# A feed-forward kernel's opening loads: the first transposed tile alone, and part of the first weights on another queue

## The chip, the cores and the metric

The kernel runs on 1 core of one Trainium2 chip. The metric is the device time of one execution in microseconds (us); the median of several runs is compared. Engines are named as in the profile: PE is TensorE's matmul, PEld its weight load, ACT ScalarE, DVE VectorE, POOL GpSimd, SP SyncE. SPq and ACTq are the DMA issues on SyncE's and ScalarE's queues.

## What is computed

```python
# x: 1 x 2048 x 640, w1: 640 x 1728, w2: 1728 x 640, all bf16
h = jnp.einsum("bsd,df->bsf", x, w1)
h = silu(h)
out = jnp.einsum("bsf,fd->bsd", h, w2)
```

## The kernel before, in words

**Tiling.** The 2048 tokens are cut into four chunks of 512. The inner size 640 is five k-tiles of 128 (`DT`). The hidden size 1728 is thirteen f-tiles of 128 (`FT`) and a rest of 64. x arrives transposed: `xT[:, k, c0:c1]` holds k-tile k of a chunk, 128 partitions by 512 tokens, and is filled by DMA transposes straight from DRAM. "Tile k" in this text is that k-tile for the first chunk. w1 lies in `w1s[:, k, f]`; "slab k" is its k-th tile, of which the first eight f-tiles (1024 columns, 256 KB) are loaded first.

**The first product.** One block is one f-tile with one k-tile: two matmuls of 64 columns of w1 each (`step`, lines 183 to 187), which run side by side into the two halves of a PSUM bank. The first chunk is special. `opening` (197 to 205) goes through the k-tiles in the outer loop and through eight f-tiles in the inner one, each f-tile in its own bank, so that work can begin when only tile 0 and part of slab 0 have landed. It waits for tile 0 and the first part of slab 0, then for the rest of slab 0 ahead of f-tile `NA`, then in `sweep` for slab and tile k. The fifth k-tile follows at 208 to 211, where each f-tile ends in a SiLU on ACT. After that come f-tiles 8 to 12 of the first chunk, and the three other chunks with the f-tile in the outer loop.

**The second product.** It reads the activated `hT` and w2 and runs on PE to the end; ACT and DVE copy the banks out, SP stores them. The change does not touch it.

**What stands before the first block.** DVE clears a small tile `z` (line 125), and PE multiplies it with itself: 13 dummies of 128 columns and 256 moving columns, and one more as two halves of 64 (`first_dummies`, 135 to 138). Their result is never used. ACT meanwhile loads its table and runs one small SiLU (`warm_up`).

**The order of the loads.** `early` moves an instruction ahead of its engine's part in the barrier at the program's start, so these loads are issued at once. SP's queue takes, in the order of lines 123 to 157: tiles 0 and 1 in one transpose; f-tiles 5 to 7 of slab 0 (`ld_w1b`); slab 1; slab 2; tile 2; slab 3; tiles 3 and 4 in one transpose; slab 4; f-tiles 8 and 9 of all slabs (`ld_rest`); the remaining columns (`ld_rest2`). ACT's queue takes f-tiles 0 to 4 of slab 0. After the barrier SP issues 15 transposes for the other chunks (163) and the loads of w2. A queue issues in its own order, and each DMA has its semaphore, for which `wait` makes an engine stand. The semaphore `s_pe` counts the work that PE announces with `tick`; before the change the dummies announce none.

Of the kernel before, what the change touches and what calls it, by code (L numbers as in the profile page):

```python
# [9 lines left out]
def bass_standalone__dense_activation_silu__prompt_kernel(  # L10
# [13 lines left out]
    P = 128  # L24
    NB = 8
    BANK = 512
    DT = D // P
    FT = F // P
    FL = F - FT * P
    SCH = 512  # L30
    HB = 256
# [7 lines left out]
    pe, act, dve, pool, sp = nc.tensor, nc.scalar, nc.vector, nc.gpsimd, nc.sync  # L39

    with ExitStack() as es:
        def sb(name, shape, dtype):
            return es.enter_context(nc.sbuf_tensor(name, shape, dtype))
# [10 lines left out]
        z = sb("z", [P, HB], bf16)  # L54
        ps = es.enter_context(nc.psum_tensor("ps", [P, NB, BANK], fp32))
# [4 lines left out]
        def sem(name):  # L60
            s = es.enter_context(nc.semaphore(name))
            count[s.name if hasattr(s, "name") else name] = 0
            return [s, 0]

        def tick(ins, s, n=1):
            ins.then_inc(s[0], n)
            s[1] += n
            return (s, s[1])

        def wait(eng, *points):  # L70
            for pt in points:
                if pt is None:
                    continue
                s, v = pt
                key = (id(eng), id(s))
                if seen.get(key, 0) < v:
                    eng.wait_ge(s[0], v)
                    seen[key] = v

        s_pe, s_act, s_dve = sem("s_pe"), sem("s_act"), sem("s_dve")  # L80
# [4 lines left out]
        def load(eng, out_ap, in_ap):  # L85
            s = sem(f"s_ld{n_dma[0]}")
            n_dma[0] += 1
            return tick(eng.dma_start(out=out_ap, in_=in_ap), s, 16)

        def turned(c0, c1, k0, k1):  # L90
            s = sem(f"s_tr{n_dma[0]}")
            n_dma[0] += 1
            return tick(sp.dma_start_transpose(
                out=xT[:, k0:k1, c0:c1], in_=xf[c0:c1, k0 * P:k1 * P]), s, 16)

        ET = mybir.EngineType

        def early(emit, engine, arrived=True):
            n = len(nc.main_func.blocks[0].instructions)
            r = emit()  # L100
            lst = nc.main_func.blocks[0].instructions
            new = lst[n:]
            del lst[n:]
            at = next(
                i for i, ins in enumerate(lst)
                if ins.opcode == ("EventSemaphore" if arrived else "Drain") and ins.engine == engine
            )
            lst[at:at] = new
            return r
# [2 lines left out]
        w2_v = w2[0:F0, :].rearrange("(ft p) d -> p ft d", p=P)  # L112

        NO = NB
        NA = 5
        CO = NO * P

        def slab(eng, k, f0=0, f1=NO):
            return load(eng, w1s[:, k, f0 * P:f1 * P], w1_v[:, k, f0 * P:f1 * P])

        ld_w1 = {}
        ld_t = {}
        ld_t[0] = ld_t[1] = early(lambda: turned(0, SCH, 0, 2), ET.SP, False)
        ld_w1[0] = early(lambda: slab(act, 0, 0, NA), ET.Activation, False)
        p_z = early(lambda: tick(dve.memset(z[:, :], 0.0), s_dve), ET.DVE, False)  # L125

# [2 lines left out]
        def dummies(n, w):  # L129
            for _ in range(n):  # L130
                for c0 in range(0, P, w):
                    pe.matmul(ps[c0:c0 + w, 3, 0:HB], lhsT=z[:, 0:w], rhs=z[:, :],  # L132
                              start=True, stop=True)

        def first_dummies():
            wait(pe, p_z)
            dummies(13, P)
            dummies(1, HC)

        p_warm = early(lambda: tick(pool.memset(warm[:, :], 0.0), s_pool), ET.Pool, False)  # L140
# [4 lines left out]

        early(warm_up, ET.Activation, False)

        ld_w1b = early(lambda: slab(sp, 0, NA, NO), ET.SP, False)
        ld_w1[1] = early(lambda: slab(sp, 1), ET.SP, False)
        ld_w1[2] = early(lambda: slab(sp, 2), ET.SP, False)  # L150
        ld_t[2] = early(lambda: turned(0, SCH, 2, 3), ET.SP, False)
        ld_w1[3] = early(lambda: slab(sp, 3), ET.SP, False)
        ld_t[3] = ld_t[4] = early(lambda: turned(0, SCH, 3, DT), ET.SP, False)
        ld_w1[4] = early(lambda: slab(sp, 4), ET.SP, False)
        CM = CO + 2 * P
        ld_rest = early(lambda: load(sp, w1s[:, :, CO:CM], w1_v[:, :, CO:CM]), ET.SP, False)
# [17 lines left out]
        def mm(o, l, r, start, stop, shared=False):  # L174
            return pe.matmul(o, lhsT=l, rhs=r, start=start, stop=stop, skip_group_check=shared)  # L175
# [7 lines left out]
        def step(b, k, ft, c0, c1, start=False, stop=False):  # L183
            for h0 in (0, HC):
                ins = mm(ps[h0:h0 + HC, b, :], w1s[:, k, ft * P + h0:ft * P + h0 + HC],
                         xT[:, k, c0:c1], start, stop, shared=True)
            return ins
# [9 lines left out]
        def opening():  # L197
            first_dummies()
            wait(pe, ld_t[0], ld_w1[0])
            for ft in range(NO):  # L200
                if ft == NA:
                    wait(pe, ld_w1b)
                part(0, ft, 0, SCH, start=True)
            for k in range(1, DT - 1):
                sweep(k, 0, SCH, ld_w1[k], ld_t[k])
# [16 lines left out]
        for ft in range(NO, FT):  # L222
# [3 lines left out]
            for k in range(DT):  # L226
                ins = step(b, k, ft, 0, SCH, start=(k == 0), stop=(k == DT - 1))
            silu(hT[:, ft, 0:SCH], ps[:, b, :], b, tick(ins, s_pe))
        for c in range(1, NSC):
            wait(pe, ld_xc[c])  # L230
            for ft in range(FT):
                b = bank()
                for k in range(DT):
                    ins = step(b, k, ft, c * SCH, (c + 1) * SCH, start=(k == 0), stop=(k == DT - 1))
                h_last = silu(hT[:, ft, c * SCH:(c + 1) * SCH], ps[:, b, :], b, tick(ins, s_pe))
        h_tail = []
        for q in range(NSC // 2):
            b = bank()
            for k in range(DT):
                for hh in range(2):  # L240
                    c = 2 * q + hh
                    ins = mm(ps[hh * FL:(hh + 1) * FL, b, :], w1s[:, k, F0:F],
                             xT[:, k, c * SCH:(c + 1) * SCH],
                             start=(k == 0), stop=(k == DT - 1), shared=True)
# [130 lines left out]
        for u, eng in ((A, dve), (B, act), (C, act), (E, dve), (G2, act)):  # L375
            for ft in range(FT):
                ins = u.whole(ft, ft == FT - 1)
# [30 lines left out]
```

## Time and profile before

| | us |
|---|---|
| median of 3 runs (lowest, highest) | 124.72 (124.39, 125.12) |
| span of the profiled execution, first to last instruction | 123.8 |
| last semaphore resets in its trace, after the first instruction | 124.7 |
| first dummy on PE | 0.39 |
| first real matmul | 3.82 |
| PE busy in all | 121.3 |

The page gives the profiled execution's span, and no other time of it. The loads that the first sweeps wait for, in that execution (issue is the start of the DMA's issue; landed is when its semaphore was full; wanted is when the first weight load that waits for it started):

| load | queue | issue us | landed us | wanted us |
|---|---|---|---|---|
| tiles 0 and 1 | SP | 0.00 | 3.78 | 3.82 |
| slab 0, f-tiles 0 to 4 (160 KB) | ACT | 0.12 | 2.86 | 3.82 |
| slab 0, f-tiles 5 to 7 (96 KB) | SP | 1.39 | 5.24 | 5.53 |
| slab 1 (256 KB) | SP | 2.00 | 5.88 | 6.52 |
| slab 2 | SP | 2.49 | 6.59 | 8.25 |
| tile 2 | SP | 2.97 | 7.15 | 8.25 |
| slab 3 | SP | 4.17 | 8.23 | 9.97 |
| tiles 3 and 4 | SP | 4.79 | 9.24 | 9.97 |
| slab 4 | SP | 6.07 | 10.55 | 11.70 |
| f-tiles 8 and 9 of all slabs | SP | 6.69 | 12.51 | 13.43 |

How to read the profile: a timeline line has the start, the time, the engine, the line of the kernel, the operation, its tiles and how many were joined; in brackets stands how long the engine was idle before and what ended that. The chain of waits is followed back from the last instruction to what released each step. Matmuls are pipelined, so a matmul's own time is longer than the distance between the starts of two.

### The profile page before, as it was taken

To read this page: it belongs to the slowest core of one execution; us is meant where nothing else is said; L and a number is where in the kernel's file an instruction comes from. 1 tells how busy PE (TensorE), PEld (TensorE's weight loads), DVE (VectorE), ACT (ScalarE), POOL (GpSimd) and SP (SyncE) were. 2 spreads that over 40 slices of the span, in tenths; PEclk is the share of its full clock that TensorE was granted. 3 is DMA by queue.
4 is the path that set the end of the run, shared out by engine and by line. 5 is a ranking of instruction groups with operands and counts; after the bars stand their busy time and mean duration, and the time that the engine had idled before them with its cause. 6 is when DMAs were issued, how large, how long until landed. Compare 5 with 4: busy or idle time off the path is not lost.

```text
span 123.8 us, 2298 instructions
## 1 busy us (share of the span) xinstructions
PE 121.3 (98%) x1056; PEld 58.9 (48%) x1057; DVE 6.9 (6%) x11; ACT 38.8 (31%) x67; POOL 0.3 (0%) x5
## 2 busy tenths in 40 slices
PE   8999999999999999999999999999999999999993
PEld 5345545545545545545544444444444444444452
DVE  0000000000000000000000022002200300222001
ACT  4000985555555555555530011001100200110110
POOL 0000000000000000000000000000000000000000
DMA  6999974554894000000000004302200220023112
GB/s 138 239 246 331 138 86 91 100 77 107 214 394 157 0 0 0 3 5 0 0 0 5 0 0 101 74 0 105 107 0 5 106 106 0 5 106 116 53 66 82
DMA packets 19625, 10.42 MB, mean 84 GB/s; under 512 B 13728, under 2 KB 19104, under 8 KB 19616
## 3 DMA queue, kind: packets, MB, share of 16 engines
q1 hardware_dynamic: 19472, 10.11, 34.1%
q10 hardware_dynamic: 144, 0.16, 0.6%
q8 instruction: 8, 0.13, 0.5%
q14 instruction: 1, 0.01, 0.0%
HBM read 4.51 MB, written 2.62 MB: 58 GB/s over the span
## 4 chain that ended last, share of the span: by engine, by line
PE 95%; DMA 3%; ACT 0%; issue 0%
PE ps L175 95%; DMA xT<-in_x_dram 3%; ACT o_sb L256 0%
## 5 line engine op out<-in xcount | busy, mean ns | idle before, releaser
L175 PE MATMUL ps<-xT,w1s 128*64 128x512 bf16 x540 | 59.6, 384 | 0.1
L175 PE MATMUL ps<-w2s,hT 64*128 64x512 bf16 (+3 forms) x376 | 46.0, 369 | 0.2 <-issue 0.2
L175 PEld LDWEIGHTS ps<-xT,w1s 128*64 128x64 bf16 x540 | 30.0, 111 | 29.6 <-issue 1.2
L179 ACT ACTIVATE hT<-ps 128x512 bf16<-128x512 f32 x52 | 30.0, 607 | 29.9 <-PE ps L175 29.9
L175 PEld LDWEIGHTS ps<-w2s,hT 64*128 64x128 bf16 (+1 forms) x377 | 21.0, 95 | 24.2 <-issue 0.2
L256 ACT CAST o_sb<-ps 128x512 bf16<-128x512 f32 (+1 forms) x9 | 5.0, 551 | 41.5 <-PE ps L175 41.5
L175 PE MATMUL ps<-hT,w2s 64*128 64x512 bf16 x104 | 11.7, 376 | 0.0
L175 PEld LDWEIGHTS ps<-hT,w2s 64*128 64x128 bf16 x104 | 5.0, 94 | 6.3 <-issue 0.4
L254 DVE CAST o_sb<-ps 128x512 bf16<-128x512 f32 (+1 forms) x8 | 5.4, 675 | 40.5 <-PE ps L175 40.5
L254 DVE CAST oT<-ps 128x512 bf16<-128x512 f32 x2 | 1.4, 692 | 74.2 <-PE ps L175 74.2
L256 ACT CAST oT<-ps 128x512 bf16<-128x512 f32 x2 | 1.2, 586 | 10.6 <-PE ps L175 10.6
L132 PE MATMUL ps<-z 128*128 128x256 bf16 (+1 forms) x15 | 3.3, 419 | 0.4 <-DVE z L125 0.4
L175 PE MATMUL ps<-w2t,hTt 64*128 64x512 bf16 (+2 forms) x17 | 2.9, 363 | 0.0
L132 PEld LDWEIGHTS ps<-z 128*128 128x128 bf16 (+1 forms) x15 | 1.9, 142 | 1.5 <-issue 0.4
L179 ACT ACTIVATE hTt<-ps 128x512 bf16<-128x512 f32 x2 | 1.2, 598 | 1.0 <-PE ps L175 1.0
L144 ACT ACT_TABLE_LOAD x1 | 1.3, 1283 | 0.5 <-issue 0.5
L175 PEld LDWEIGHTS ps<-w2t,hTt 64*128 64x128 bf16 x17 | 0.9, 94 | 1.1
L175 PE MATMUL ps<-hTt,w2t 64*128 64x512 bf16 x4 | 0.8, 376 | 0.0
L175 PEld LDWEIGHTS ps<-hTt,w2t 64*128 64x128 bf16 x4 | 0.2, 94 | 0.2
L144 ACT ACTIVATE warm<-warm 128x32 f32<-128x32 f32 x1 | 0.2, 229 | 0.0
L125 DVE MEMSET z<- 128x128 uint32 x1 | 0.2, 165 | 0.2 <-issue 0.2
L140 POOL MEMSET warm<- 128x32 f32 x1 | 0.1, 125 | 0.0
(4 smaller groups left out, 0.4 us busy)
## 6 DMA issues: line engine op xcount, KB each, us to landing
out_dram<-o_sb SPq DMA_DIRECT2D x15, 160.0 KB, 1.8
w2s<-in_w_dram SPq DMA_DIRECT2D x1, 1120.0 KB, 6.1
w1s<-in_w_dram SPq DMA_DIRECT2D x4, 256.0 KB, 4.1
w2s<-in_w_dram SPq DMA_DIRECT2D x1, 960.0 KB, 8.2
w1s<-in_w_dram SPq DMA_DIRECT2D x1, 560.0 KB, 7.0
w1s<-in_w_dram SPq DMA_DIRECT2D x1, 320.0 KB, 5.8
xT<-in_x_dram SPq DMA_TRANSPOSE x18, 3.7
w1s<-in_w_dram ACTq DMA_DIRECT2D x1, 160.0 KB, 2.7
```

What stands on the lines that cost most here:

```text
L125: p_z = early(lambda: tick(dve.memset(z[:, :], 0.0), s_dve), ET.DVE, False)
L132: pe.matmul(ps[c0:c0 + w, 3, 0:HB], lhsT=z[:, 0:w], rhs=z[:, :], start=True, stop=True)
L140: p_warm = early(lambda: tick(pool.memset(warm[:, :], 0.0), s_pool), ET.Pool, False)
L144: act.activation(out=warm[:, :], in_=warm[:, :], func=ACT.Silu)
L175: return pe.matmul(o, lhsT=l, rhs=r, start=start, stop=stop, skip_group_check=shared)
L179: r = tick(act.activation(out=out_ap, in_=in_ap, func=ACT.Silu), s_act)
L254: r = tick(dve.tensor_copy(out=out_ap, in_=in_ap), s_dve)
L256: r = tick(act.copy(out=out_ap, in_=in_ap), s_act)
```

## The change

The pair of tiles 0 and 1 becomes tile 0 alone; tiles 1 and 2 go in one transpose right behind it on SP's queue. ACT's first load of slab 0 has four f-tiles, not five. The other four f-tiles of slab 0, and slab 1, move from SP's queue to ACT's, behind a wait for the fourth dummy, which now announces itself on `s_pe`. Three whole dummies go: 4 and 6 stand where 13 stood, and the one in two halves stays.

```diff
-        NA = 5
+        NA = 4
...
-        ld_t[0] = ld_t[1] = early(lambda: turned(0, SCH, 0, 2), ET.SP, False)
+        p_gate = (s_pe, 1)
+        ld_t[0] = early(lambda: turned(0, SCH, 0, 1), ET.SP, False)
...
-                    pe.matmul(ps[c0:c0 + w, 3, 0:HB], lhsT=z[:, 0:w], rhs=z[:, :],
-                              start=True, stop=True)
+                    ins = pe.matmul(ps[c0:c0 + w, 3, 0:HB], lhsT=z[:, 0:w], rhs=z[:, :],
+                                    start=True, stop=True)
+            return ins
...
-            dummies(13, P)
+            assert tick(dummies(4, P), s_pe) == p_gate
+            dummies(6, P)
             dummies(1, HC)
...
-        ld_w1b = early(lambda: slab(sp, 0, NA, NO), ET.SP, False)
-        ld_w1[1] = early(lambda: slab(sp, 1), ET.SP, False)
+        early(lambda: wait(act, p_gate), ET.Activation, False)
+        ld_w1b = early(lambda: slab(act, 0, NA, NO), ET.Activation, False)
+        ld_w1[1] = early(lambda: slab(act, 1), ET.Activation, False)
+        ld_t[1] = ld_t[2] = early(lambda: turned(0, SCH, 1, 3), ET.SP, False)
         ld_w1[2] = early(lambda: slab(sp, 2), ET.SP, False)
-        ld_t[2] = early(lambda: turned(0, SCH, 2, 3), ET.SP, False)
         ld_w1[3] = early(lambda: slab(sp, 3), ET.SP, False)
-        ld_t[3] = ld_t[4] = early(lambda: turned(0, SCH, 3, DT), ET.SP, False)
+        ld_t[3] = ld_t[4] = early(lambda: turned(0, SCH, 3, 5), ET.SP, False)
```

## The prediction

> **What bounds the kernel now.** I read three views, in this order: the page's chain, the timeline of the weight loads, and the timeline of SyncE's queue. The page's chain says which engine sets the end.
>
> ```profile
> PE 95%; DMA 3%; ACT 0%; issue 0%
> PE ps L175 95%; DMA xT<-in_x_dram 3%; ACT o_sb L256 0%
> ```
>
> The same chain in order of time (start us, us, what) says where PE begins:
>
> ```profile
> 0.00 3.78 DMA xT<-in_x_dram
> 3.78 0.04 issue
> 3.82 106.78 PE ps L175 x706
> ```
>
> The reader is to see that after 3.82 us nothing but PE stands on the path, and before it one transfer, the transpose of tiles 0 and 1 (landed 3.78). So the change can act only on when the first real matmul starts, on how fast the first matmuls run, and on new waits in PE. The weight loads' timeline (start us, us) shows the second point:
>
> ```profile
> 3.27 0.13 PEld L132 LDWEIGHTS ps<-z 128*64 128x64 bf16 x2 [0.41 <-issue]
> 3.82 0.18 PEld L175 LDWEIGHTS ps<-xT,w1s 128*64 128x64 bf16 x4 [0.42 <-DMA xT<-in_x_dram]
> 4.25 0.18 PEld L175 LDWEIGHTS ps<-xT,w1s 128*64 128x64 bf16 x2 [0.25 <-issue]
> ...
> 5.53 0.18 PEld L175 LDWEIGHTS ps<-xT,w1s 128*64 128x64 bf16 x2 [0.25 <-DMA w1s<-in_w_dram]
> 5.96 0.18 PEld L175 LDWEIGHTS ps<-xT,w1s 128*64 128x64 bf16 x2 [0.25 <-issue]
> 6.30 7.67 PEld L175 LDWEIGHTS ps<-xT,w1s 128*64 128x64 bf16 x72 [0.17 <-issue]
> ```
>
> A block is one f-tile with one k-tile, a pair of 64-column matmuls side by side. Until 5.96 the blocks start 0.427 us apart; from 6.30 on they start 0.216 us apart. One block, at 5.96, takes 0.343 and lies across the switch, which I put at T = 6.13. The granted clock stands at 1.00 in every stretch, so no column shows this; the spacing does. PE began its dummies at 0.39, so the slow stretch lasted 5.74 us. SyncE's queue (start us, us, of DMA issues) shows what holds the rest of the loads:
>
> ```profile
> 0.00 1.33 SPq L93 DMA_TRANSPOSE xT<-in_x_dram  x1
> 1.39 1.54 SPq L88 DMA_DIRECT2D w1s<-in_w_dram  x3
> 2.97 1.16 SPq L93 DMA_TRANSPOSE xT<-in_x_dram  x1
> 4.17 0.58 SPq L88 DMA_DIRECT2D w1s<-in_w_dram  x1
> 4.79 1.24 SPq L93 DMA_TRANSPOSE xT<-in_x_dram  x1
> 6.07 1.62 SPq L88 DMA_DIRECT2D w1s<-in_w_dram  x3
> 8.09 3.83 SPq L163 DMA_TRANSPOSE xT<-in_x_dram  x2
> ```
>
> A transpose costs the queue 1.16 us for one tile and 1.24 to 1.33 for two, so its issue hardly depends on the tiles; its packets do.
>
> **The change, part by part.** The page gives the profiled execution no time of its own. Its span is 123.8, and the last semaphore resets in the trace come 124.7 us after the first instruction; that equals the median of the three runs, 124.72, so I count from 124.72.
>
> *Tile 0 alone.* The pair: issue 1.33, 1024 packets of 256 bytes from 1.76 to 3.32, landed 3.78. One tile has half the packets. Low bound: transposes of one tile that read DRAM later in the trace land at best 2.7 us after issue, with 2.9 twice. High bound: the pair's 3.78. In the trace 439 of the pair's packets had begun by 2.50 with slab 0's five blocks beside them; 512 would have gone by about 2.6, and the pair's own last packet landed 0.46 after it went, which gives 3.05 as an estimate. Slab 0's first part is now four blocks, not five (128 KB for 160 KB), which frees some of that, so I take 2.9 for the landing, nearest to the uncontended 2.9 rows.
>
> *Three dummies fewer.* Dummies start 0.213 apart. The 13th began at 2.93 and the two halves at 3.28; three fewer put the halves at 2.64 and their end of issue 0.21 later, at 2.85. So PE is free at 2.85, the tile is there at 2.9, slab 0's first part by 2.86 or earlier (five blocks landed at 2.86). First real matmul S = 2.95 (landing plus the 0.04 of the chain), against 3.82: 0.87 us earlier. Bounds: 2.85 to 3.8.
>
> *What 0.87 us is worth.* If T stays, the extra time is spent at the slow rate: 0.87 / 0.427 = 2.04 more blocks are done by T, and each saves 0.216 of full-rate time: 0.44 us. If T comes earlier by as much, all 0.87 us count. I take 0.44: the activity that precedes T began with the first dummy at 0.39, which does not move. Full-array dummies or real blocks fill PE in both kernels; the gap of 0.12 ahead of 3.82 becomes some 0 to 0.1.
> The Trainium skill ("TensorE: Matmul & The Clock Gate", Part 1, "What's actually happening") says that PE starts at half clock and gets the full one after a busy window of about 3.4 us, and that the windows run freely, whenever the kernel starts. The trace's 5.74 us agrees only if a window's edge fell inside the dummies. By that page the switch falls by chance in each run, and half of any earlier start is lost, the 0.44 above; the other sum, 0.87, is rival 1's.
>
> *Rest of slab 0 and slab 1 on ScalarE.* The wait is for the 4th dummy, which began at 1.01 and took 0.42: the gate opens at about 1.45. ScalarE's own table load and first activation (0.52 to 2.05) run in the engine while its sequencer was free (its drain stood waiting from 0.59). So the two loads are issued at about 1.5 and 2.0, against 1.39 and 2.00 on SyncE. If they had to wait for the activation instead, they go at 2.1 and 2.6. Queued behind the wait are these two issues, ScalarE's arrival at the barrier (late is 7.75, SyncE's), and the first activation at 12.34: nobody is late. On SyncE these loads stood in the queue behind the pair; the first landed at 5.24 (3.9 from issue). On ScalarE slab 0's first part took 2.7 beside the pair. So the rest of slab 0 lands at 4.2 (bounds 4.2 and 5.4). PE wants it for the fifth block, 2.95 + 4 x 0.427 = 4.66: margin 0.45, or a stall of 0.75 at the far bound. Slab 1 lands at 4.7 to 6.1 (2.7 to 4.1 from issue) and is wanted at about 6.2, when the eighth block ends. No cost taken.
>
> *Tiles 1 and 2 at once.* Issued at about 1.25, land 3.8 to 4.5 us later (the two pairs of the trace), 5.0 to 5.75; tile 1 wanted at 6.2. Margin 0.45 or more. The Trainium skill ("DMA: Bandwidth & Descriptors", "Issuing engines are not separate DMA queues") says that queues of different engines share the same 16 DMA engines and only issue time is saved. By it the pair shares with slab 1, which is why I keep 5.75 as an end; no number above uses it.
>
> *The rest of SyncE's queue.* It loses two copies (0.56 and 0.45) and one separate transpose (1.16), and the first transpose gets about 0.15 shorter, while tile 2 rides with tile 1: 1.1 us shorter with the gaps. Slabs 2, 3, 4, tiles 3 and 4, the two last pieces of w1, and the 15 transposes after the barrier (now at about 7.0, not 8.09) all go some 1.1 earlier, while PE wants them 0.44 earlier. In the old trace none was late: slab 2 landed 6.59 for 8.25, slab 4 10.55 for 11.70, chunk 1's tiles 18.02 for 18.82. So margins grow and no new wait opens.
>
> Sum: 124.72 - 0.44 = **124.28 us**.
>
> **Rivals.**
> 1. *The switch moves with the real matmuls* (zeros not counting as activity, or the 0.12 gap having spoiled something): T = 6.13 - 0.87 and all of it counts: 123.85. For it: from 3.82 to 6.13 is a stretch too; against: dummies keep PE as busy as blocks in the busy column (2.33 of 2.33 us from 0.39 to 2.72).
> 2. *The fifth block waits* (slower). The rest of slab 0, on its new queue beside the transposes, lands after 4.66, at 5.4 as it would at its old 3.9 us. The stall of 0.75 costs 0.37 at half rate and breaks PE's busy stretch. If the stretch then had to start again, T would be 5.4 + 5.74 = 11.1, not 6.13; every us of that costs half. Between no delay and 5.0 us I take 2.5: 124.28 + 0.37 + 1.25 = 125.9. It decides once that landing passes 4.66. Against: 2.7 us for the row on the same queue.
> 3. *The start does not move*: the fixed 1.16 of issue and slab 0's packets hold tile 0 until 3.6 or later, so S = 3.65 and 0.08 is won: 124.6.
>
> **How the numbers follow.** Forecast 0.44, rival 1 0.28, rival 2 0.17, rival 3 0.11. The three runs before lie 0.73 apart, so a median is uncertain by about 0.3; the forecast's own range is 124.0 to 124.6. Half a per cent is 0.62 us, about what a measurement of this kernel can tell from no change. Below 124.10: rival 1 nearly whole (0.27) and 0.13 of the forecast: 0.40. Above 125.34: rival 2, 0.16. Within: 0.44. The range leaves out most of rival 2 and a tail of rival 1: 123.6 to 124.9.
>
> **What would show it.** In the changed profile: the first L179 weight load near 2.95 (right), at 3.6 or later (rival 3). Spacing 0.427 until about 6.1 (right), until about 5.3 (rival 1), later than 7 (rival 2). A weight load that waits for w1s at the fifth block: rival 2. A wait for xT at the ninth block would show tiles 1 and 2 late, which I deny. Any idle PE after the first 13 us makes the argument on margins wrong.

## The result

The changed kernel takes 125.90 us (median of 6 runs, 125.11 to 126.19) against 124.62 for the kernel before (6 runs, 124.39 to 125.12): a ratio of 1.0092, interval 1.0066 to 1.0117. It is slower, by about 1.2 us; 124.28 had been forecast.

The profiled execution took 126.19 with a span of 124.8. In every run of the changed kernel time and span differ by 1.3 to 1.4 us, so the 123.8 of the profile before belongs to a run of about 125.1, not to the median. A second profile of the kernel before shows that: span 123.8, time 125.10.

The chain of the changed kernel in order of time (start us, us, what):

```profile
0.00 1.23 SPq L93
1.23 0.05 issue
1.29 6.29 DMA xT<-in_x_dram
7.57 0.14 issue
7.71 115.28 PE ps L179 x1025
```

The transfer at the head of the chain is now the second transpose, tiles 1 and 2, issued at 1.29 and landed 6.29 us later; before, it was the first, landed at 3.78. The weight loads' timeline (start us, us, and the idle time before) shows the same from PE's side:

```profile
3.13 0.18 PEld L179 LDWEIGHTS ps<-xT,w1s 128*64 128x64 bf16 x4 [0.38 <-DMA xT<-in_x_dram]
...
4.64 0.38 PEld L179 LDWEIGHTS ps<-xT,w1s 128*64 128x64 bf16 x4 [0.47 <-DMA w1s<-in_w_dram]
5.27 0.18 PEld L179 LDWEIGHTS ps<-xT,w1s 128*64 128x64 bf16 x2 [0.25 <-issue]
5.70 0.18 PEld L179 LDWEIGHTS ps<-xT,w1s 128*64 128x64 bf16 x2 [0.25 <-issue]
7.68 8.37 PEld L179 LDWEIGHTS ps<-xT,w1s 128*64 128x64 bf16 x80 [1.80 <-DMA w1s<-in_w_dram]
```

The first real matmul starts at 3.14 instead of 3.82. The fifth block needs the rest of slab 0 at 4.64 and gets it (landed 4.60): the weight load waits a little, the matmuls go on 0.427 apart. Then the second sweep stands until 7.68. The row names w1s, since slab 1's wait stands on the weight load itself; slab 1 had landed at 7.35, and the pair of tiles, for which PE's sequencer stood just before, at 7.57. The timeline of the matmuls names the pair:

```profile
7.71 6.67 PE L179 MATMUL ps<-xT,w1s 128*64 128x512 bf16 x60 [1.32 <-DMA xT<-in_x_dram]
```

Sum of the two profiles: PE reached the end of its eighth block 0.51 us earlier than before (6.22 for 6.74; 0.69 of start at the slow spacing gives 0.35, a switch to the fast spacing at 5.88 and not 6.2 the rest), then waited 1.49. That is 0.97 later into the second sweep, and 0.97 later into the second round of f-tiles. From block 41 to the end of the span both kernels take 110.2 us. So the whole difference is made before the second sweep.

SyncE's queue after the change (start us, us, of DMA issues):

```profile
0.00 2.57 SPq L93 DMA_TRANSPOSE xT<-in_x_dram  x2
2.62 1.05 SPq L88 DMA_DIRECT2D w1s<-in_w_dram  x2
3.71 1.41 SPq L93 DMA_TRANSPOSE xT<-in_x_dram  x1
5.16 2.97 SPq L88 DMA_DIRECT2D w1s<-in_w_dram  x3
8.55 2.46 SPq L167 DMA_TRANSPOSE xT<-in_x_dram  x2
```

Neither the pair (1.29) nor slab 1 (1.82, on ScalarE's queue) was issued late; the transfers themselves are slow. Slab 1's 128 packets of 2048 bytes started between 4.60 and 6.70 and took 192 ns on average (median 89); before, the first 128 of that size started between 3.35 and 4.93 and took 120 (median 84). The stretches (us, PEclk, DMA share, GB/s) show the hole, first in the changed kernel, then in the one before:

```profile
4.00:5.00 1.00, 1.00 1.38 228
5.00:6.00 1.00, 1.00 0.89 134
```

```profile
4.00:5.00 1.00, 1.00 0.88 294
5.00:6.00 1.00, 1.00 1.48 330
```

The engines moved 134 GB/s where they had moved 330, just when PE was about to need both loads.

### The profile page after: what moved, and what is told of

The parts are those of the page before. It is cut to its first block, busy times and chain, and to the rows that moved or that the text cites. A ratio compares the mean times of both kernels' runs of the same rounds, so it can differ in the third digit from the quotient of the medians.

```text
span 124.8 us, 2293 instructions
## 1 busy us (share of the span) xinstructions
PE 121.2 (97%) x1054; PEld 66.3 (53%) x1054; DVE 7.0 (6%) x11; ACT 38.8 (31%) x67; POOL 0.3 (0%) x5
## 3 DMA queue, kind: packets, MB, share of 16 engines
HBM read 4.51 MB, written 2.62 MB: 57 GB/s over the span
## 4 chain that ended last, share of the span: by engine, by line
PE 92%; DMA 5%; SPq 1%; ACT 0%; issue 0%
PE ps L179 92%; DMA xT<-in_x_dram 5%; SPq L93 1%; ACT o_sb L260 0%
## 5 line engine op out<-in xcount | busy, mean ns | idle before, releaser
L179 PEld LDWEIGHTS ps<-xT,w1s 128*64 128x64 bf16 x540 | 37.8, 112 | 23.4 <-DMA w1s<-in_w_dram 2.3
L133 PE MATMUL ps<-z 128*128 128x256 bf16 (+1 forms) x12 | 2.7, 419 | 0.4 <-DVE z L126 0.4
```

The costliest lines, as they stand in the source:

```text
L133: ins = pe.matmul(ps[c0:c0 + w, 3, 0:HB], lhsT=z[:, 0:w], rhs=z[:, :], start=True, stop=True)
```

## The experiments

The experiments take the opening apart. Theory A: copies on the second queue and transposes on the first slow each other while both run. Theory B: a pair of tiles behind tile 0 is late whatever runs beside it. Theory D, formed after the first four runs: tile 2's bytes, sent ahead of their need, are the trouble, by the pair's joint semaphore or by standing in front. The landings and the start of the second sweep in each kernel's profiled run, with the times of all its runs (the ratio is to the kernel before, on the same chip):

| kernel | tile 1 landed | slab 1 landed | second sweep | median us | ratio, interval |
|---|---|---|---|---|---|
| before | 3.78 | 5.88 | 6.74 | 124.62 | |
| changed | 7.57 | 7.35 | 7.71 | 125.90 | 1.0092 (1.0066, 1.0117) |
| k1 one queue, pair | 6.09 | 5.10 | 6.23 | 124.79 | 1.0014 (0.9992, 1.0036) |
| k2 slab 1 behind the pair | 5.26 | 6.71 | 6.75 | 125.59 | 1.0068 (1.0044, 1.0093) |
| k3 two queues, split | 5.63 | 5.43 | 6.06 | 124.57 | 1.0003 (0.9983, 1.0024) |
| k4 no gate | 6.38 | 5.38 | 7.10 | 126.05 | 1.0104 (1.0050, 1.0157) |
| k5 queue move alone | 3.32 | 6.39 | 6.53 | 125.42 | 1.0104 (1.0051, 1.0157) |
| k6 two queues, two singles | 6.03 | 5.70 | 6.39 | 124.79 | 1.0018 (0.9994, 1.0042) |
| k7 one queue, split | 6.11 | 5.09 | 6.25 | 125.77 | 1.0102 (1.0066, 1.0137) |
| k8 split, late start | 5.82 | 5.60 | 6.32 | 125.01 | 1.0041 (1.0015, 1.0067) |
| k9 split, no gate | 5.45 | 4.94 | 6.14 | 125.73 | 1.0103 (1.0067, 1.0138) |
| k10 split, whole slab 0 first | 6.22 | 5.75 | 6.48 | 124.83 | 1.0023 (1.0000, 1.0046) |
| k11 slab 0's rest back | 5.83 | 4.72 | 5.97 | 124.79 | 1.0029 (1.0004, 1.0053) |
| k12 slab 1 issued later | 5.13 | 8.53 | 8.57 | 128.20 | 1.0122 (1.0062, 1.0181) |
| k13 slab 2 behind slab 1 | 6.54 | 6.31 | 6.67 | 125.39 | 1.0058 (1.0036, 1.0080) |
| k14 k11, split | 5.47 | 4.92 | 6.08 | 125.17 | 1.0051 (1.0031, 1.0070) |

A landing is that of one profiled run and varies from run to run; the medians are the better witness. The start of the second sweep also holds the eight blocks ahead of it, and with them the moment at which the spacing falls from 0.427 to 0.216. Only in some of these runs did PE stand still just ahead of it: 1.49 us in the changed kernel, 3.17 in k12, 1.33 in k2 and k13, 0.6 in k1 and k7, under 0.1 in k11 (the distance from the eighth block's start to the ninth's, less 0.216). In the others the blocks run on (in k6 the 0.383 between the two starts is a block at the slow spacing, up to the switch).

### Both kernels profiled again

l1_changed_again: the changed kernel unaltered. Expected:

> The changed kernel unaltered, a second look. If the pair beside slab 1 is late in every run, both land past 6.9 us and the second sweep starts past 7, whenever the block spacing goes from 0.427 to 0.216. If the first look was an accident of that run, the pair lands near 5.5 and the second sweep starts by 6.4.

Measured: 125.01 us, the pair at 6.42, slab 1 at 6.20, second sweep at 6.56. Neither end: late, but by 1.15 less. One of the six runs above was like it (125.11), five lay at 125.83 to 126.19. A run without any wait, started at 3.1 and switched as late as the 6.2 of the kernel before, would end near 3.1 + 40 x 0.216 + (6.2 - 3.1)/2 + 110.2 + 1.3 = 124.8, so those five hold a wait of about 1 us, if they switched no later than that (k4's profiled run, below, switched near 7.3).

l2_before_again: the kernel before unaltered. Expected:

> The kernel before unaltered, a second look. If the switch of the spacing falls by chance, it lies elsewhere than at 6.13 us (between 4 and 7.3), and the time differs by half of the shift; the pair lands at 3.7 to 3.8 again and the first real matmul starts at 3.8 again. If it is tied to the program, the switch is at 6.1 again.

Measured: 125.10 us, pair at 3.63, first matmul 3.68, six blocks at the slow spacing with the switch near 6.2 again. Alone it would have spoken for a fixed switch; the other profiles below speak against.

### Pair and second queue, each without the other

k1_one_queue, the pair without the second queue:

```diff
-        early(lambda: wait(act, p_gate), ET.Activation, False)
-        ld_w1b = early(lambda: slab(act, 0, NA, NO), ET.Activation, False)
-        ld_w1[1] = early(lambda: slab(act, 1), ET.Activation, False)
+        ld_w1b = early(lambda: slab(sp, 0, NA, NO), ET.SP, False)
+        ld_w1[1] = early(lambda: slab(sp, 1), ET.SP, False)
         ld_t[1] = ld_t[2] = early(lambda: turned(0, SCH, 1, 3), ET.SP, False)
```

> The rest of slab 0 and slab 1 go back to SyncE's queue, behind tile 0 and ahead of tiles 1 and 2; no wait on ScalarE; the rest as changed. Theory A (two queues at once: the pair's packets and slab 1's interleave and both crawl): the pair of tiles, issued about 2.4 us, lands about 6.2 (3.8 from issue), the second sweep starts near 6.5, time 124.3 to 124.7. Theory B (a pair of tiles behind tile 0 is late whatever lies beside it, 6.3 us from issue as in the changed kernel): it lands near 8.7, PE waits 2 us, time 126.5 or more.

Measured 124.79, just past theory A's range: the pair landed 3.7 us from issue. Theory B falls: a pair behind tile 0 is not late in itself.

k3_split and k6_two_singles, the second queue without the pair:

```diff
 # k3_split
-        ld_t[1] = ld_t[2] = early(lambda: turned(0, SCH, 1, 3), ET.SP, False)
+        ld_t[1] = early(lambda: turned(0, SCH, 1, 2), ET.SP, False)
         ld_w1[2] = early(lambda: slab(sp, 2), ET.SP, False)
+        ld_t[2] = early(lambda: turned(0, SCH, 2, 3), ET.SP, False)
 # k6_two_singles
-        ld_t[1] = ld_t[2] = early(lambda: turned(0, SCH, 1, 3), ET.SP, False)
+        ld_t[1] = early(lambda: turned(0, SCH, 1, 2), ET.SP, False)
+        ld_t[2] = early(lambda: turned(0, SCH, 2, 3), ET.SP, False)
```

> Tiles 1 and 2 as two transposes (tile 1, slab 2, tile 2, slab 3 on SyncE's queue); ScalarE's queue as changed. Theory A: slab 1 still meets transposes; tile 1 lands near 5, slab 1 at 6 to 7, second sweep 6.3 to 7, time 124.6 to 125.3. Theory B: half the packets cure it, second sweep at 6.3 as soon as PE is free, time 124.3.

> The changed kernel with tiles 1 and 2 as two transposes one behind the other, same queues. Theory D, the joint semaphore: tile 1 lands by about 5.7 as in the split kernel, slab 1 by 5.5, time 124.5 to 124.8. Theory A, both queues crawl while transposes and slab 1 run side by side: tile 1 may land by 6, slab 1 still lands past 6.8 because tile 2's packets run beside it, time 125.4 or more.

Measured 124.57 and 124.79. k6 sends the same bytes in the same order on the same queues as the changed kernel; only the one transpose is two. Its tile 1 landed at 6.03 and its tile 2 at 6.21, so it isn't merely that PE waits for a joint semaphore: the whole group is done earlier than the pair. With k3 this also ends theory A as it stands: copies and transposes run side by side in both, and the time is that of the kernel before. k6's weight loads, and its matmuls:

```profile
4.51 0.41 PEld L180 LDWEIGHTS ps<-xT,w1s 128*64 128x64 bf16 x4 [0.45 <-DMA w1s<-in_w_dram]
5.16 0.18 PEld L180 LDWEIGHTS ps<-xT,w1s 128*64 128x64 bf16 x2 [0.24 <-issue]
5.58 0.18 PEld L180 LDWEIGHTS ps<-xT,w1s 128*64 128x64 bf16 x2 [0.24 <-issue]
6.13 3.40 PEld L180 LDWEIGHTS ps<-xT,w1s 128*64 128x64 bf16 x32 [0.36 <-issue]
```

```profile
3.02 11.29 PE L180 MATMUL ps<-xT,w1s 128*64 128x512 bf16 x86
```

Where the changed kernel's weight loads have a hole of 1.80 there is one of 0.36, and the matmuls have none: they run on from 3.02, and the eighth block, begun at 6.01, fills the time to the ninth at 6.39. In the packets one difference is plain: the second tile was issued only at 2.59, and slab 1's packets mostly went between 4.25 and 5.0, after tile 1's and before tile 2's. In the changed kernel, behind the pair, they began at 4.60 and met slab 2 on the other queue from 5.67.

k7_one_queue_single: neither the pair nor the second queue.

```diff
 # k1_one_queue, and
-        ld_t[1] = ld_t[2] = early(lambda: turned(0, SCH, 1, 3), ET.SP, False)
+        ld_t[1] = early(lambda: turned(0, SCH, 1, 2), ET.SP, False)
         ld_w1[2] = early(lambda: slab(sp, 2), ET.SP, False)
+        ld_t[2] = early(lambda: turned(0, SCH, 2, 3), ET.SP, False)
```

> Tile 0 alone and then everything on SyncE's queue: rest of slab 0, slab 1, tile 1, slab 2, tile 2, slab 3; no wait on ScalarE, 10 dummies. Theory A: nothing runs side by side; tile 1 lands near 5.7, second sweep near 6.2, time 124.2 to 124.5. Rival: the first blocks' early start is worth nothing, since the loads bound the second sweep: 124.5 to 124.8.

Measured 125.77, a miss for both. The second sweep starts as early as in k1 (6.25 and 6.23). What is late comes behind: a fourth transpose of 1.1 to 1.3 us stands in SyncE's queue beside all the copies, tiles 3 and 4 are issued at 5.98 (4.79 before) and land at 10.23, and PE's weight loads stand for chunk 1's tiles until 20.2. The waits of PE's weight loads in the first 22 us (total, times, longest) hold the second of these:

```profile
PEld ps L179 <- DMA xT<-in_x_dram: 1.1, 1, 1.1
```

So joining two tiles, or moving copies off SyncE, buys queue time, and as far as these kernels go one of the two is needed.

### What stands on ScalarE's queue

k5_old_tiles: the queue move alone, with the tiles and the 13 dummies of before.

```diff
 # against the changed kernel
-        ld_t[0] = early(lambda: turned(0, SCH, 0, 1), ET.SP, False)
+        ld_t[0] = ld_t[1] = early(lambda: turned(0, SCH, 0, 2), ET.SP, False)
...
-            dummies(6, P)
+            dummies(9, P)
...
-        ld_t[1] = ld_t[2] = early(lambda: turned(0, SCH, 1, 3), ET.SP, False)
         ld_w1[2] = early(lambda: slab(sp, 2), ET.SP, False)
+        ld_t[2] = early(lambda: turned(0, SCH, 2, 3), ET.SP, False)
```

> Only the move of the rest of slab 0 and of slab 1 to ScalarE's queue behind the gate; tiles 0 and 1 in one transpose, tile 2 later, 13 dummies, as before the change. Theory A (two queues at once slow both): slab 0's rest meets the end of the pair, PE starts near 4.0 to 4.2, slab 1 lands by 5.5, time 124.6 to 124.9. Theory D (the trouble is tile 2's bytes sent ahead of slab 1, which this kernel doesn't have): nothing is late, 124.4 to 124.6.

Measured 125.42, past both, so theory D is not the whole of it: no tile 2 goes ahead here, and the loads are late all the same. Slab 2 had moved up to 1.39 on SyncE's queue and landed at 5.77; slab 0's rest, wanted at about 5.1, landed at 5.59 and slab 1 at 6.39. What is wanted last came before what is wanted first.

k2_slab1_back: slab 1 on SyncE's queue behind the pair.

```diff
-        ld_w1[1] = early(lambda: slab(act, 1), ET.Activation, False)
         ld_t[1] = ld_t[2] = early(lambda: turned(0, SCH, 1, 3), ET.SP, False)
+        ld_w1[1] = early(lambda: slab(sp, 1), ET.SP, False)
```

> Only slab 1 goes back to SyncE's queue, behind the pair of tiles 1 and 2; the rest of slab 0 stays on ScalarE behind the gate. Theory A: beside 128 KB instead of 384 KB the pair lands near 5.5, slab 1 behind it near 6.5, second sweep near 6.6, time 124.4 to 124.8. Theory B: the pair still lands past 7, slab 1 at 8, time 126.0 or more.

Measured 125.59. The pair is now early (5.26), but slab 1, behind it in one queue and with nothing beside it, lands only at 6.71. The expected landing of slab 1 (6.5) was near; its price was not.

k11_slab0_back and k14_split_slab0_back: only slab 1 on ScalarE's queue, with the pair and with single tiles.

```diff
 # k11_slab0_back
-        ld_w1b = early(lambda: slab(act, 0, NA, NO), ET.Activation, False)
+        ld_w1b = early(lambda: slab(sp, 0, NA, NO), ET.SP, False)
 # k14_split_slab0_back: the same, and the tiles as in k3_split
```

> The changed kernel with the rest of slab 0 on SyncE's queue between tile 0 and the pair; only slab 1 stays on ScalarE behind the gate. If slab 1 is the copy that delays the pair, the pair (issued 0.6 us later, at 1.9) lands past 6.5 and slab 1 past 6: 125.4 or more. If the rest of slab 0 on the second queue is, slab 1 lands by 5.2, the pair by 6.0: 124.5 to 124.8.

> Both cures together: rest of slab 0 on SyncE's queue behind tile 0, then tile 1, slab 2, tile 2; only slab 1 on ScalarE behind the gate. Ahead of the second sweep stand no bytes but its own: slab 1 lands by 4.8, tile 1 by 5.5, the fifth block waits to 4.9; second sweep by 5.8 to 6.1, time 124.2 to 124.5. If the wait of the fifth block (near 5.0, as with slab 0's rest there before) takes back what the second sweep wins: 124.6 to 124.9.

k11 measured 124.79: slab 1 had no other copy ahead of it on its queue, its packets went before the pair's, and it landed at 4.72, the pair at 5.83; only the fifth block had to wait, until 5.0. So slab 1 does not hurt the pair by the second queue alone; the two are late when slab 1 stands behind slab 0's rest there and so runs beside the pair. k14, meant to beat both kernels, measured 125.17: fifth block at 5.19 and then tiles 3 and 4 late (10.07), as in k7.

k12_late_slab1: slab 1's issue held to 2.74.

```diff
+        p_gate2 = (s_pe, 2)
...
-            dummies(6, P)
+            assert tick(dummies(6, P), s_pe) == p_gate2
...
+        early(lambda: wait(act, p_gate2), ET.Activation, False)
         ld_w1[1] = early(lambda: slab(act, 1), ET.Activation, False)
```

> The changed kernel with slab 1 held until the tenth dummy is through (issue at 2.75 us, not 1.82). In the changed kernel slab 1's first packet went at 4.6 anyway, so if it is the packets that meet, nothing changes: 125.7 to 126.1. If slab 1's descriptors, waiting in the second queue, already delay the pair, the pair lands near 5.3 as where slab 1 went behind it, slab 1 near 6.5: 125.0 to 125.5.

Measured 125.47 to 128.49 in five runs. In the profiled run the pair landed early, as the second case had it (5.13). With k2 (5.26) that makes two kernels whose pair is early once slab 1 isn't issued at 1.82 beside it. But slab 1 then ran beside slab 2 all the way and both ended late, 8.53 and 8.71. PE stood 3.2 us, and its clock fell. The stretches (us, PE busy, granted clock) are cut at the records of the clock:

```profile
4.48:7.89 3.41, 1.09 (x10) 1.00 1.29 235
7.89:11.31 3.42, 2.74 (x14) 0.50 0.90 237
11.31:14.00 2.69, 2.69 (x28) 1.00 1.17 335
```

Its ratio in the table is that of the two runs in which the clock did not fall so.

k13_slab2_behind: slab 2 on ScalarE's queue behind slab 1.

```diff
-        ld_w1[2] = early(lambda: slab(sp, 2), ET.SP, False)
+        ld_w1[2] = early(lambda: slab(act, 2), ET.Activation, False)
```

> The changed kernel with slab 2 on ScalarE's queue behind slab 1, so that it can't run beside slab 1. If slab 2, wanted only for the third sweep, takes half of slab 1's share in the changed kernel: slab 1 lands near 6.2, not 7.35, the pair by 6, time 125.2 to 125.5. If slab 2 has no part in it: slab 1 and the pair past 7 again, 125.8 to 126.1.

Measured 125.39, within the first case's range, and slab 1 landed at 6.31; the pair, at 6.54, lies between the first case's 6 and the second's 7. As the medians stand, about 0.4 us of the 1.2 are gone (1.0058 for 1.0092). That slab 2 is the reason isn't shown: the two intervals overlap, and the changed kernel's second profile has much the same landings (6.20 and 6.42) with slab 2 on the other queue.

### The gate, the start and the size of the first load

k4_no_gate and k9_split_no_gate take away ScalarE's wait, in the changed kernel and in k3.

```diff
-        early(lambda: wait(act, p_gate), ET.Activation, False)
```

> The changed kernel without ScalarE's wait for the fourth dummy: the rest of slab 0 and slab 1 are issued at about 0.6 and 1.0 us. Theory A: they now meet tile 0 and not the pair: tile 0 lands at 3.4 to 3.8, the pair at 5.5, second sweep near 6.6, time 124.5 to 125.0. Theory B: the pair lands past 7 as before, time 125.9 or more.

> The split kernel (tile 1 and tile 2 as two transposes, 124.57) without ScalarE's wait for the fourth dummy. If the gate's part is to keep tile 0 clear of the copies: tile 0 lands near 3.6 (2.81 in the split kernel), slab 1 near 5.0, time 124.5 to 124.9, the late start costing at most a quarter to a half of 0.8 us. If the copies lose more by meeting a transpose than tile 0 does: 125.3 or more, as in the changed kernel without its gate.

Measured 126.05 and 125.73. Tile 0 landed at 3.65 and 3.50 (3.09 and 2.81 with the gate). In the changed kernel taking the gate away makes no clear difference (1.0104 for 1.0092). In the split kernel the gate is worth about 1.2 us (125.73 for 124.57), more than the 0.7 of start; what its other runs lost was not seen, because the profiled run of k9 was by far its fastest (124.56, the others 125.52 to 126.73).

The profiled run of k4 (125.63) shows one way to lose time without any late load. Its matmuls, and two rows of its weight loads:

```profile
3.69 5.63 PE L178 MATMUL ps<-xT,w1s 128*64 128x512 bf16 x34 [0.63 <-DMA xT<-in_x_dram]
```

```profile
6.68 0.18 PEld L178 LDWEIGHTS ps<-xT,w1s 128*64 128x64 bf16 x2 [0.24 <-issue]
7.10 1.95 PEld L178 LDWEIGHTS ps<-xT,w1s 128*64 128x64 bf16 x18 [0.24 <-issue]
```

Slab 1 (5.38) and the pair (6.38) are there before PE wants them, and no load holds it up behind the first block. The blocks stay 0.427 apart until 7.10, so the switch lies near 7.3, 1.1 later than in the kernel before, which costs the 0.5 us between the two spans. PE stood idle for 0.63 us ahead of its first block. That this gap put the switch off, in k4 and in the other runs of k9, is a rival to late loads here; neither is shown.

k8_late_start: k3 with 18 whole dummies.

```diff
-            dummies(6, P)
+            dummies(14, P)
```

> The split kernel (124.57) with 18 whole dummies for 10, which puts off the first real matmul by 1.7 us (2.85 to about 4.55) and leaves every load where it was. If an earlier start counts by half, as at the slow clock, 0.85 us are lost: 125.4. If the loads bound the second sweep, much less: 124.6 to 124.9. If the start counted in full: 126.3.

Measured 125.01: a start put off from 2.85 to 4.56 costs 0.44 us, 0.26 per us of start and not 0.5, as the medians stand. The two intervals together leave room from almost nothing to 0.5.

k10_whole_slab0: k3 with the whole of slab 0 in the first load and two more dummies.

```diff
-        NA = 4
+        NA = NO
...
-            dummies(6, P)
+            dummies(8, P)
...
-        ld_w1b = early(lambda: slab(act, 0, NA, NO), ET.Activation, False)
```

> The split kernel with the whole of slab 0 in ScalarE's first load, only slab 1 behind the gate, 12 whole dummies. If the loads of the second sweep bound the opening, slab 1 with one load less ahead of it lands near 5 and tile 1 near 5.2, first real matmul at 3.4, time 124.1 to 124.4, below both kernels. If the start at 3.4 in place of 2.85 counts more: 124.6 to 124.9.

Measured 124.83, the second case: slab 1 and tile 1 did not land sooner (5.75 and 6.22).

## Why the prediction was wrong, point by point

- **Right: the early start.** Tile 0 landed at 3.09 (2.9 taken), first matmul 3.14 (2.95 taken, within 2.85 to 3.8), the gate opened at 1.46 (1.45), the rest of slab 0 landed at 4.60 (4.2 taken, 4.66 the deadline). The issues on ScalarE went during its table load, as argued.
- **Right: where the time could go.** All of it lies before the second sweep; the 110.2 us from block 41 on are the same, so the margins of the later loads held.
- **Wrong, and the step that failed:** "Slab 1 lands at 4.7 to 6.1 ... No cost taken", and "Tiles 1 and 2 at once ... 5.0 to 5.75 ... Margin 0.45 or more". They landed at 7.35 and 7.57 in the first profile and 6.20 and 6.42 in the second, and PE waited for them at the ninth block, the sign that the prediction named and denied. Both figures were taken from rows in which the load ran in another company: slab 1's 2.7 to 4.1 us from a load at the head of ScalarE's queue and from SyncE's single file, the pair's 3.8 to 4.5 from rows beside which ScalarE's queue had at most the 160 KB of slab 0. Here slab 1 stood behind slab 0's rest, which shared with the pair, and its own packets shared with the pair's last ones and with slab 2, which SyncE no longer held behind it.
- **Wrong: the queue moved past.** The prediction let everything behind the pair on SyncE's queue go 1.1 us earlier and counted that as margin. Slabs 3 and 4 and tiles 3 and 4 did go 0.9 to 1.1 earlier. Slab 2 did not (2.62, before 2.49): the two copies that left the queue ahead of it made room for the pair's 1.28. The transposes after the barrier, forecast for 7.0, went at 8.55 and 7.41 in the two profiles (8.09 before). What changed for slab 2 is that slab 1 no longer stood ahead of it: wanted at 8.25, it ran beside slab 1, wanted at 6.2. k13 would put about a third of the loss on that, which its interval doesn't settle; in k12, where the two ran side by side all the way, both landed past 8.5. k2 (slab 1 behind the pair in one file: 125.59) shows that slab 1 is also late when it stands behind the pair.
- **Rival 2 gave 125.9, by another mechanism.** In the profiled run it was the ninth block that waited, not the fifth, and the switch to the fast spacing came earlier than before (5.88), not later. The agreement of the number is chance.
- **Half of the early start.** Where the loads are in time (k3), 0.97 us of start against the first profile of before should have given 0.48; the median is 1.0003 of before (0.9983 to 1.0024). k8 finds 0.26 per us, with the room said there. An argument that fits, not shown: in runs with an early switch the second sweep waits for its loads anyway, which were there at 5.88 before and at 5.63 in k3's profile.
- **The switch.** The prediction read it at 6.13; the 0.343 of the block that lies across it, shared between 0.427 and 0.216, gives 6.22, and its sum doesn't hang on that. It said that the switch falls by chance in each run. That holds: the records of the granted clock in six profiles put it at 4.48 (k12), 4.63 (k8), 4.67 (k1), 5.03 (k5), 5.29 (k9) and 5.88 (changed), with the first dummy at 0.38 or 0.39 in all. k12's records stand 3.413 us apart, and in the other five the full clock lasted 119.47 us, 35 times that. The Trainium skill ("TensorE: Matmul & The Clock Gate", Part 1, "What's actually happening") has free-running windows of 3413 ns, and these traces agree. A switch that falls anywhere in such a window makes the times of one kernel differ by up to 1.7 us, half the window, as an estimate; the 107 runs of the kernel before that stand beside the experiments, on five chips, lie between 123.80 and 125.46.

Part of the pair's delay lies behind its last packet. In the 18 profiles every transpose of the first chunk was full 0.45 to 0.6 us after its last packet had gone, except eight, which took 1.0 to 1.5. In those eight, and in no other, a copy on ScalarE's queue was still under way, begun at least 0.3 us before that packet. The pair of the changed kernel is one of them (last packet through at 6.28, full at 7.57; in the second profile 5.21 and 6.42), and so is tile 0 without the gate: its last packet was through at 2.62 in k4 and 2.48 in k9, 2.62 and 2.36 with the gate. Tile 1 of k3, k6 and k8 belongs to them too, but one tile's packets are through by 4.3 to 4.5. This is a pattern over profiles; no run was made to test it.

What stays open: what holds such a transpose back, why single packets of 2048 bytes took 192 ns on average, and why the pair's last packets came as late as 6.3 when a queue of copies ran beside it. k6 shows that one transpose as two is enough to bring the time back to that of the kernel before; why the packets then go sooner was not found. That the length of the wait differs between runs of one kernel (125.0 and 125.9) was not explained either, nor how much of it is a later switch. The Trainium skill ("DMA: Bandwidth & Descriptors", "Issuing engines are not separate DMA queues") says that DMAs of several engines interleave on the same 16 and save only issue time. The runs agree that no bandwidth was won (134 GB/s between 5 and 6 us, 330 before), and here interleaving lost time.

## What to carry to other kernels

Within one queue, the loads of these runs landed in the order of their issue, which can be the order in which they are wanted; on two queues they land as the two happen to share, so a load that is wanted later must not be let loose beside one that is wanted now. Before a load is moved, list for each sweep the bytes that will be on their way ahead of its last one, on all queues, and take a landing time only from a row with the same company. A start won in the opening counts only up to the next load that binds, and at the slow spacing (0.427 for 0.216) by half at most.

## What the runs showed that was not expected

- A transpose costs its queue mostly 1.1 to 1.3 us of issue whether it has one tile or two. Splitting the pair made the transfers no slower (k6) but costs the queue a second issue, which k7 and k14 could not spare.
- A transpose can be complete in its packets and still be late: beside a copy on the other queue its semaphore was full 1.0 to 1.5 us after its last packet, and not 0.45 to 0.6.
- An idle PE soon loses its clock: in k12 PE was busy 1.09 of a 3.41 us window, and ran the whole next one at a granted clock of 0.50; after that window, busy for 2.74 of 3.42, it had the full clock again.
- Holding a load back can be worth more than sending it early: ScalarE's wait for the fourth dummy saves about 1.2 us in the split kernel, though nothing clear in the changed one.
